# A new order for the first 480 entries of a hand-ordered gated-attention and MLP kernel, with GpSimd's steps there on VectorE

## The chip, the cores and the metric

One core of a Trainium2 chip runs the whole kernel. TensorE multiplies matrices into PSUM, VectorE and ScalarE work element by element, GpSimd is another element-wise engine, and SyncE (SP) issues the DMA transfers. Each engine takes its instructions from a queue of its own, strictly in the order in which the program issued them, and waits at an instruction until the data of other engines is there. The metric is the device time of one execution in microseconds; the median of three runs counts.

## The reference

```python
def _attn_ref(q, k, v, f_logit):            # 4 x 8 heads, 768 steps, 48 wide
    f = 1.0 / (1.0 + np.exp(-f_logit))
    for t in range(S):
        state = f[:, :, t, :, None] * state + einsum('bhd,bhe->bhde', k[:, :, t], v[:, :, t])
        y[:, :, t] = einsum('bhd,bhde->bhe', q[:, :, t], state)

def _moe_ref(x, w_in, w_out):               # 3072 tokens, 384 -> 2048 -> 384
    h = x @ w_in
    g = h * np.clip(h + 3.0, 0.0, 6.0) / 6.0
    return g @ w_out
```

The output of the gated attention, reshaped to 3072 tokens of 384 numbers, is the input `x` of the MLP.

## The kernel before

The sequence of 768 steps is cut into 6 chunks of 128, so there are 24 units (4 batches, 6 chunks); unit `i` is batch `i % 4` of chunk `i // 4`, and the units of one chunk make up one group of 512 tokens for the MLP. The state of each batch is carried from chunk to chunk.

A unit runs through these steps, each named in the order list with the unit's number. SP loads its gates (`load`), queries and keys (`loadq`) and values (`loadv`). ScalarE takes the sigmoid (`gate`). VectorE scans the gates backwards (`back`, line 428) and multiplies the keys (`kmul`, line 441), takes the reciprocal of the chunk's decay (`rend`, lines 444 and 445), scans forwards (`fwd`, line 448) and multiplies the queries (`qmul`, line 454). TensorE transposes the keys (`tk`, line 516; ScalarE copies the result, `ktok`), makes the keys-by-values products (`kv`, line 537), the queries-by-keys products (`att`, line 497), which VectorE masks (`mask`, line 504), and from them and the state the output (`qs`, line 571, and `av`, line 587). `carry0`, `carry1` and `decay` (line 457) pass the state on, from chunk 1 on by VectorE. ScalarE copies the output as a 16-bit number (`xh`); `xs` (line 612, TensorE) and `xl` add its rest for the first units; `hole` is a DMA that moves some rows of it.

The weights arrive in 16 blocks (`ld.f`, 768 KB each) and are turned into a 16-bit upper part and a 16-bit rest by ScalarE (`z`, `cy`, `high`) and VectorE (`mid`, line 301, `dif`, line 308, `top`, line 312, and `low`, or its halves `lowi` and `lowo`, line 320).

The MLP of block `f` for a group is `mm1` (9 matmuls, TensorE), `relu` (ScalarE), `g` (VectorE), `gh` (ScalarE) and `gl` (VectorE, line 693) and `mm2` (9 matmuls). For the first blocks of the first group it is cut in halves of two units each: `mm1a`, `relua`, `ga` (line 841), `mm2a` for units 0 and 1, and the same with `b` for units 2 and 3. In the first group, `mm2a`, `mm2b` and `mm2x` read the 32-bit weights. `warm.n` multiplies a blank tile into an unused bank, n times 128 columns (line 1071); its result is read by nobody.

The order of all this is a list written out in the program: `ORDER`, 1559 entries. An entry is a step, its number and, for steps that write to one of the five PSUM banks shared by attention and MLP, the bank (0 to 3 the halves of two pairs, 4 the single one; for `att`, `kv` and `qs` the number says which half of which pair). The loop at line 1063 calls the steps in the list's order, and lines 1088 and following hold each engine's queue to it. The order of two entries on different engines doesn't matter, except through banks and buffers. Gates have 3 buffers, so `load.3` waits until unit 0's scans are done, and `load.4` until unit 1's are; raw weights have 3 buffers, queries and values 4. `ON_POOL` names the steps that `engine()` (line 373) puts on GpSimd instead of VectorE; there are 15, all in the first 433 entries.

Of the kernel before, what the change touches and what calls it, by code (L numbers as in the profile page):

```python
# [63 lines left out]
mm2a.1 ktok.4 loadv.4 ld.3 cy.3 z.3 hole.2 mid.2 dif.2 top.2 att.4.2 kv.4.3 hole.3 mm1b.0.0 high.2 back.5 mid.3  # L64
relub.0 loadq.5 mm1b.1.1 relub.1 lowi.2 gb.0 dif.3 kmul.5 rend.5 gb.1 mm1a.2.4 mm1b.2.0 top.3 mm2b.0 mm2b.1 fwd.5
tk.5.1 relua.2 relub.2 gb.2 qmul.5 ld.4 z.4 cy.4 mid.4 mm2b.2 high.3 ktok.5 lowi.3 ga.2 mm1b.3.0 load.6 gate.6 loadq.6
dif.4 back.6 top.4 load.7 mm1a.3.4 ld.5 relub.3 mm2a.2 relua.3 ga.3 high.4 gb.3 cy.5 z.5 mask.4 mm2a.3 lowi.4 mm1a.4.1
relua.4 rend.6 ld.6 mm1b.4.4 relub.4 loadv.6 gate.7 loadq.7 mm2b.3 carry0.4 kmul.6 fwd.6 mid.5 ga.4 dif.5 z.6 qmul.6
top.5 cy.6 tk.6.1 ktok.6 mm2a.4 back.7 ld.7 decay.5 high.5 qs.4.2 decay.6 att.5.0 gb.4 av.4 kv.6.1 carry1.4 lowi.5
mm1.5.4 mask.5 mm2b.4 carry0.6 xh.4 z.7 xl.4 mid.6 dif.6 kmul.7 carry1.6 loadv.5 kv.5.3 ld.8 relu.5 g.5 mm2x.5 cy.7  # L70
top.6 high.6 cy.8 rend.7 tk.7.0 mid.7 dif.7 load.8 lowi.6 carry0.5 top.7 mm1.6.4 ktok.7 qs.5.2 fwd.7 qmul.7 high.7
loadv.7 relu.6 g.6 z.8 decay.7 att.6.0 ld.9 lowi.7 gate.8 av.5 cy.9 z.9 mask.6 mm1.7.4 relu.7 mid.8 dif.8 top.8 mid.9
carry1.5 dif.9 high.8 low.8 mm2x.6 mm1.8.0 g.7 loadq.8 ld.10 top.9 xh.5 cy.10 relu.8 high.9 back.8 rend.8 mm2x.7 ld.11
xl.5 g.8 att.7.2 z.10 cy.11 qs.6.0 kv.7.3 mid.10 load.10 loadv.8 av.6 dif.10 low.9 top.10 z.11 mid.11 gh.8 mm1.9.4
ld.12 ld.14 xh.6 xl.6 gl.8 mm2.8 dif.11 high.10 low.10 relu.9 g.9 cy.12 mm1.10.1 top.11 mask.7 kmul.8 carry0.7 gh.9
gl.9 hole.4 relu.10 high.11 mm2.9 carry1.7 g.10 low.11 z.12 mid.12 ld.13 dif.12 top.12 cy.13 gh.10 gl.10 tk.8.1 ktok.8
mm1.11.0 z.13 high.12 qs.7.2 mm2.10 av.7 loadq.9 ld.15 kv.8.3 decay.8 relu.11 mid.13 dif.13 low.12 loadv.9 mm1.12.1
g.11 gh.11 xh.7 top.13 carry0.8 high.13 xl.7 hole.7 gl.11 relu.12 z.14 z.15 low.13 fwd.8 qmul.8 mm2.11 g.12 gh.12
mm1.13.4 relu.13 g.13 cy.14 gh.13 gl.13 gl.12 mm2.12 cy.15 qs.8.2 mid.14 dif.14 att.8.0 mask.8 lowo.0 top.14 high.14
hole.6 hole.5 mm1.16.4 load.9 mid.15 mm1.17.1 relu.16 carry1.8 relu.17 dif.15 ws1.0 g.16 mm1.20.0 g.17 loadq.11 low.14  # L80
gate.10 xtop.0 gate.9 mm1.18.1 load.11 top.15 relu.18 loadq.10 back.9 high.15 gh.16 av.8 back.10 mm1.14.4 g.18 mm2.13
lowo.4 gh.17 relu.14 low.15 g.14 gh.14 mm1.15.1 mm1.19.4 lowo.6 gh.18 kmul.9 gl.18 rend.9 relu.15 g.15 lowo.3 gh.15
# [1 line left out]
mm2.16 gate.11 lowo.2 ws2.0 relu.19 od.0 ws3.0 mm2.17 rend.10 xh.8 g.19 back.11 od.2 kmul.10 relu.20 decay.9 relu.23
kmul.11 hole.8 fwd.10 rend.11 od.1 load.13 qmul.10 xsum.0.2 g.20 g.23 mm1.21.4 relu.21 load.12 xleast.0 tk.10.3 ws4.0
qmul.9 decay.10 ktok.10 mm2.18 gh.19 g.21 mm1.25.3 gh.20 mm1.24.2 gh.21 loadv.10 gate.12 wtop.4 gl.19 relu.24 att.9.1
relu.25 kv.9.0 gl.20 fwd.11 g.25 carry0.9 loadv.12 g.24 wsh.0 load.14 qmul.11 mm1.22.4 gate.13 relu.22 back.12 gh.24
mm2.19 tk.11.3 gl.21 ws1.1 mask.9 gh.23 carry1.9 ktok.11 mm2.20 g.22 qs.9.0 att.11.3 gate.14 loadq.12 gh.25 gl.25 av.9
att.10.2 mm2.21 back.13 gh.22 xh.9 gl.23 kv.11.0 rend.12 kv.10.1 gl.22 mask.10 loadq.13 decay.11 mm1.26.4 ws2.1
mask.11 carry0.10 qs.10.3 ws3.1 carry0.11 carry1.10 kmul.12 kmul.13 fwd.12 qs.11.1 av.10 av.11 relu.26 mm2.22 ws4.1  # L90
xh.10 xh.11 decay.12 rend.13 mm1.27.3 gl.24 carry1.11 relu.27 loadq.14 decay.13 fwd.13 tk.12.2 mm1.28.1 relu.28 hole.9
ktok.12 wsl.0 ws1.2 g.27 tk.13.0 mm2.23 qmul.12 qmul.13 wsh.1 hole.10 att.13.3 ws2.2 g.26 ktok.13 g.28 xtop.1 att.12.1
t0.4 loadv.13 kv.12.2 kv.13.0 back.14 carry0.13 load.15 hole.11 load.16 xsum.1.4 carry0.12 gh.26 mm2.24 gh.27 mm2.25
t0.5 mask.13 carry1.12 t1.4 t1.5 seed.0.2 kmul.14 mm1.30.3 gh.28 t2.4 ws3.2 xleast.1 carry1.13 t2.5 th.4 ws4.2 gate.15
mask.12 gl.26 gl.27 wsl.1 th.5 ws1.3 mm2.26 tl.4 mm1.29.1 tk.14.2 relu.30 mm1.31.0 tl.5 relu.29 rend.14 g.30 p1.8.4
loadv.14 ktok.14 ws2.3 relu.31 p7.8.2 g.29 wsh.2 cs.8 ca.8.2 loadv.17 mm2.27 g.31 p6.8 gh.29 gate.16 fwd.14 qs.13.0
xtop.2 cx.8.3 qs.12.1 p2.8 wsl.2 ws3.3 ra.8 back.15 gl.28 p5.8 av.13 av.12 mm2.28 gh.31 gaw.8 loadq.15 loadq.17 gh.30
ws4.3 rend.15 load.17 ce.8 wsh.3 p4.8 qmul.14 gl.30 gl.29 xh.13 xh.12 p3.8 p8.8 rb.8 rx.8 p7.9.1 decay.14 wsl.3 mm2.29
gl.31 kmul.15 loadq.16 re.8 tk.15.0 gew.8 cs.9 p1.9.4 gbw.8 ca.9.2 mm2.30 fwd.15 loadv.15 gxw.8 back.16 ktok.15
xsum.2.1 mm2.31 p6.9 qmul.15 p7.11.0 xmost.2 gh.33 gh.34 cs.11 xleast.2 p2.9 decay.15 gl.34 hole.13 gh.32 kv.15.1  # L100
kv.14.0 kmul.16 cx.9.3 gl.32 outs.5 load.18 ra.9 hole.12 carry0.14 carry1.14 p4.9 carry0.15 outs.3 carry1.15 p5.9 rx.9
att.14.0 gaw.9 att.15.1 ce.9 outv.4 gate.17 p8.9 mask.14 rend.16 p3.9 mask.15 gh.35 gate.18 qs.15.0 back.17 re.9
qs.14.1 gxw.9 fwd.16 kmul.17 gl.33 gl.35 mm2.32 av.14 av.15 gew.9 p7.10.3 xh.15 rend.17 loadq.18 mm2.33 mm2.34 t0.6
p1.10.4 rb.9 mm2.35 gbw.9 qmul.16 fwd.17 xh.14 loadv.16 back.18 gh.37 gh.38 rend.18 cs.10 decay.16 load.19 kmul.18
ca.10.2 gl.38 hole.15 p6.10 gh.36 tk.17.0 gl.37 p2.10 hole.14 decay.17 tk.16.1 gh.39 cx.10.3 gl.36 p4.10 t1.6 gate.19
fwd.18 ra.10 gaw.10 t2.6 ktok.17 p5.10 ktok.16 att.16.0 kv.16.1 mm2.36 ce.10 t0.7 qmul.17 p8.10 load.20 rx.10 re.10
load.21 qmul.18 back.19 loadv.18 p3.10 mm2.37 rb.10 mask.16 gew.10 carry0.16 carry1.16 p1.11.4 gbw.10 gh.40 att.17.0
gxw.10 kv.17.1 t1.7 th.6 loadq.19 ca.11.2 gl.40 gl.39 mm2.38 gh.42 p6.11 t2.7 carry0.17 xtop.3 carry1.17 gl.42 gate.21
wtop.3 th.7 p2.11 rend.19 tl.6 mm2.39 cx.11.3 gate.20 mm2.40 mask.17 ra.11 gaw.11 tl.7 p4.11 gh.43 rx.11 p5.11 ce.11
tk.18.1 p7.13.0 p8.11 gh.41 gxw.11 gl.43 ktok.18 cs.13 gl.41 xsum.3.3 wtop.8 p3.11 qs.17.1 rb.11 qs.16.0 mm2.41  # L110
loadq.20 re.11 av.17 xmost.3 loadv.19 av.16 xleast.3 p7.12.3 gbw.11 gh.46 gew.11 xh.16 gh.45 p1.12.4 ca.12.2 xh.17
gl.45 mm2.42 loadv.23 att.18.1 kv.18.0 decay.18 gh.44 p2.12 p6.12 back.20 gl.46 cs.12 mm2.43 cx.12.3 carry0.18 gl.44
# [1126 lines left out]
```

## Time and profile before

| what | value |
|---|---|
| median of 3 runs | 459.32 us (459.2 to 459.85) |
| the profiled execution | 459.1 us, of which 457.4 us are its span |
| TensorE matmuls, busy | 449.4 us, 98% of the span |
| VectorE, busy | 359.3 us, 79% |
| ScalarE, busy | 231.2 us, 51% |
| GpSimd, busy | 19.0 us, 4%, all in the first 105 us |

The span is the time from the first to the last instruction of that one execution. [...] The letters at an idle time name the engine and line that ended it.

### The profile page before, as it was taken

Reading aid. Unit: us, or ns where it says so; the run is one execution under the profiler, and the core shown is the slowest. Engines: PE = TensorE matmul, PEld = TensorE weight load, DVE = VectorE, ACT = ScalarE, POOL = GpSimd, SP = SyncE. Lnnn points to the kernel's source line nnn. Section 1 sums busy time; section 2 is a strip of 40 time slices with the busy share of each in tenths; the row PEclk is TensorE's granted clock in tenths of the full one; section 3 lists DMA queues with packets and bytes.
Section 4 is the critical chain, followed back from the end, with each engine's and each line's share of the span. In section 5 each row is a group of like instructions: output and inputs, shape, how many; then the busy total and the mean of one; then the engine's idle time right before and its main releaser. Section 6 shows DMA issues by size and latency. Waiting matters only on the chain.

```text
span 457.4 us, 12555 instructions
## 1 busy us (share of the span) xinstructions
PE 449.4 (98%) x5445; PEld 292.8 (64%) x5449; DVE 359.3 (79%) x643; ACT 231.2 (51%) x389; POOL 19.0 (4%) x31
## 2 busy tenths in 40 slices
...
GB/s 283 223 251 385 225 189 251 203 155 16 52 125 99 158 52 59 108 3 120 89 1 85 78 142 18 21 143 2 1 10 1 5 29 2 1 115 2 1 0 73
DMA packets 25531, 43.18 MB, mean 94 GB/s; under 512 B 2560, under 2 KB 17408, under 8 KB 25472
## 3 DMA queue, kind: packets, MB, share of 16 engines
...
q10 hardware_dynamic: 1600, 0.79, 0.6%
q14 instruction: 16, 0.13, 0.1%
...
## 4 chain that ended last, share of the span: by engine, by line
PE 94%; DVE 2%; DMA 1%; ACT 1%; issue 0%; SPq 0%; ACTq 0%
PE o L709 35%; PE pair L772 16%; PE single L772 9%; PE pair L664 7%; PE single L664 5%; PE o L846 3%; PE pair L497 3%; PE pair L587 3%; PE pair L571 3%; PE pair L537 2%; PE o L720 2%; PE pair L516 2%; PE o_half L862 1%; PE pair L862 1%; PE single L828 1%; PE pair L828 1%
## 5 line engine op out<-in xcount | busy, mean ns | idle before, releaser
L709 PE MATMUL o<-gg,weight 128*128 128x512 f16 x744 | 173.5, 379 | 0.1
L709 PEld LDWEIGHTS <-weight 128*128 128x128 f16 x744 | 71.7, 98 | 73.8
L772 PEld LDWEIGHTS <-weight 128*128 128x128 f16 x672 | 65.1, 98 | 13.3 <-issue 0.2
L772 PE MATMUL pair<-xmem,wide 128*128 128x256 f16 x384 | 51.2, 273 | 0.1
L683 ACT ACTIVATE gg<-raws 128x512 f16<-128x512 f32 x64 | 38.4, 624 | 23.9 <-DVE raws L806 8.1
L772 PE MATMUL single<-xmem,weight 128*128 128x256 f16 x384 | 49.8, 273 | 0.2 <-DVE raws L806 0.2
L801 ACT ACTIVATE raws<-pair,half 128x512 f32<-128x512 f32 x32 | 21.5, 684 | 42.7 <-PE pair L772 33.7
L772 PEld LDWEIGHTS <-wide 128*128 128x128 f16 x384 | 36.9, 98 | 8.7 <-DVE single L787 0.6
L801 ACT ACTIVATE raws<-single,half 128x512 f32<-128x512 f32 x32 | 22.0, 687 | 40.0 <-PE single L772 32.4
L664 PEld LDWEIGHTS <-weight 128*128 128x128 f16 x243 | 23.1, 98 | 26.8 <-issue 0.3
L772 PE MATMUL pair<-xmem,weight 128*128 128x256 f16 x288 | 36.5, 273 | 0.0
L806 DVE SCALAR_TENSOR_TENSOR raws<-raws,single 128x512 f32<-128x512 f32 x32 | 21.8, 682 | 18.4 <-ACT raws L801 18.4
L693 DVE TENSOR_TENSOR gg<-raws,gg 128x512 f16<-128x512 f32 x48 | 31.9, 682 | 5.0 <-ACT gg L683 5.0
L664 PE MATMUL pair<-xmem,weight 128*128 128x512 f16 x144 | 33.2, 379 | 0.0
L787 DVE TENSOR_TENSOR pair<-pair,raws 128x512 f32<-128x512 f32 x16 | 11.2, 697 | 25.5 <-PE pair L772 17.2
L806 DVE SCALAR_TENSOR_TENSOR raws<-raws,pair 128x512 f32<-128x512 f32 x32 | 21.5, 681 | 12.3 <-ACT raws L801 12.1
L448 DVE TENSOR_TENSOR_SCAN suffix<-gates,rend 112x516 f32<-112x516 f32 x24 | 29.7, 1236 | 0.1
L428 DVE TENSOR_TENSOR_SCAN suffix<-gates,unit 112x516 f32<-112x516 f32 x23 | 28.1, 1224 | 0.5 <-ACT gates L422 0.5
L664 PE MATMUL single<-xmem,weight 128*128 128x512 f16 x99 | 23.2, 380 | 0.1
L674 ACT ACTIVATE tg<-pair,half 128x512 f32<-128x512 f32 x16 | 10.9, 687 | 19.5 <-PE pair L664 16.3
L683 ACT ACTIVATE gg<-tg 128x512 f16<-128x512 f32 x24 | 14.4, 626 | 9.1 <-DVE tg L678 5.2
L504 DVE TENSOR_TENSOR a<-pair,causal 128x512 f32<-128x512 f32 x24 | 16.3, 682 | 1.2 <-PE pair L537 1.2
...
## 6 DMA issues: line engine op xcount, KB each, us to landing
qkf<-qk SPq DMA_DIRECT2D x24, 512.0 KB, 4.9
...
```

The lines of the kernel that those rows point to most:

```text
L428: nc.vector.tensor_tensor_scan(flat(sf)[:, ::-1], gt[:, 1:][:, ::-1], flat(unit)[:, ::-1], 0.0, op0=ALU.mult, op1=ALU.add,)
L448: nc.vector.tensor_tensor_scan(flat(sf), gt[:, :NP * (C + 1)], flat(rend), 0.0, op0=ALU.mult, op1=ALU.add,)
L497: nc.tensor.matmul(d["at"][HC * odd:HC * (odd + 1), e, 2 * n + c], t[rs, 1, n, c, odd], t[rs, 0, n, c, odd], start=not growing[at], stop=T ...
L504: nc.vector.tensor_tensor(d["a"].rearrange("r p e t -> r e p t"), d["at"], causal.unsqueeze(1).unsqueeze(1).broadcast_to([128, 2, NP, HC]) ...
L571: nc.tensor.matmul(d["y"][to:to + 64, odd, n, cs], before[rs, p], t[rs, 0, n, c, odd], start=alone and (odd, e) not in seen, stop=False, s ...
L664: nc.tensor.matmul(h, win[:, f, a, k * 128:(k + 1) * 128], g["xt"][:, k, :g["n"] // C, b], start=i == 0, stop=i == 3 * KT - 1,)
L683: nc.scalar.activation(d["gg"][:, 0], d["t"], AF.Copy)
L693: engine("gl", int(g["name"]) * NF + f).tensor_tensor(d["gg"][:, 1], d["t"], d["gg"][:, 0], op=ALU.subtract)
L709: nc.tensor.matmul(g["o"][m], wout[:, f, a, m * 128:(m + 1) * 128], g[f]["gg"][:, b], start=f == 0 and i == 0, stop=f == NF - 1 and i == 2 ...
L772: nc.tensor.matmul(to[:, n * 256:(n + 1) * 256], weights(q, n, a), g["wide"][:, :, block - 3, b], start=fresh and count == 1, stop=count = ...
L801: nc.scalar.activation(to, src, AF.Relu, bias=half, scale=RISE)
L806: nc.vector.scalar_tensor_tensor(to, to, TOP, src, op0=ALU.min, op1=ALU.mult)
```

## The change

`ON_POOL` is emptied, so its 15 steps go to VectorE: `kmul` of units 1, 6, 7 and 8, `qmul` of unit 8, `decay` of units 4, 7 and 8, three `gl`, and four of the weights' steps. The first 471 entries of `ORDER` are replaced by 480. They are the same steps in another order and partly with other banks; only the warm entries differ, where one `warm.5` goes and ten `warm.1` are added (44 units of 128 columns in place of 39). From `mm2.14` on, 1088 entries are unchanged. The beginning and the last line of both parts:

```diff
 ON_POOL = """
-kmul.1 decay.4 kmul.6 lowi.5 kmul.7 decay.7 lowi.7 kmul.8 gl.9 decay.8 gl.11 qmul.8 gl.12 lowo.0 low.14
+
 """.split()
 ORDER = """
-load.0 loadh.0 gate.0 gateh.0 back.0 backh.0 loadq.0 loadv.0 rend.0 kmul.0 load.1 fwd.0 gate.1 back.1 warm.16 tk.0.3
-ktok.0 warm.4 kv.0.1 carry0.0 load.2 qmul.0 warm.1 att.0.0 loadq.1 ld.0 rend.1 qs.0.2 mask.0 gate.2 warm.1 av.0 xh.0
-kmul.1 tk.1.4 ktok.1 carry1.0 fwd.1 qmul.1 warm.3 att.1.0 xs.0 loadv.1 back.2 mask.1 rend.2 cy.0 load.3 warm.3 kv.1.3
-z.0 mid.0 loadq.2 gate.3 back.3 ld.1 carry0.1 warm.1 qs.1.0 dif.0 kmul.2 top.0 fwd.2 xl.0 carry1.1 loadq.3 av.1 hole.0
-tk.2.4 rend.3 xh.1 xs.1 xl.1 z.1 qmul.2 warm.5 att.2.2 kmul.3 cy.1 mid.1 fwd.3 ktok.2 loadv.2 high.0 warm.4 kv.2.1
-carry0.2 tk.3.4 ktok.3 mask.2 load.4 gate.4 qs.2.0 hole.1 av.2 xh.2 carry1.2 lowi.0 mm1a.0.4 relua.0 dif.1 qmul.3
-top.1 high.1 ga.0 loadv.3 xs.2 att.3.2 mask.3 kv.3.1 ld.2 carry0.3 carry1.3 lowi.1 xl.2 loadq.4 warm.1 qs.3.2 av.3
-xh.3 mm1a.1.4 cy.2 xs.3 xl.3 relua.1 z.2 back.4 kmul.4 rend.4 fwd.4 ga.1 decay.4 mm2a.0 qmul.4 load.5 gate.5 tk.4.1
...
-gl.14 gl.15 tk.9.1 lowo.5 lowo.1 mm2.14 fwd.9 mm2.15 gl.16 ktok.9 gl.17 outs.2 loadv.11 lowo.7 outv.1 outs.0 mm1.23.1
...
+load.0 loadh.0 gate.0 gateh.0 back.0 backh.0 loadq.0 loadv.0 rend.0 kmul.0 load.1 fwd.0 warm.16 loadq.1 tk.0.2 gate.1
+ktok.0 warm.4 warm.1 back.1 qmul.0 kmul.1 loadq.2 load.2 warm.1 kv.0.3 carry0.0 gate.2 warm.1 rend.1 att.0.1 tk.1.4
+loadv.2 loadv.1 mask.0 warm.3 load.3 fwd.1 warm.1 back.2 ktok.1 qmul.1 warm.1 carry1.0 ld.0 gate.3 kmul.2 qs.0.1
+kv.1.3 load.4 av.0 rend.2 loadq.3 carry0.1 att.1.2 back.3 xh.0 tk.2.4 z.0 carry1.1 qs.1.0 mask.1 warm.1 warm.1 gate.4
+ktok.2 warm.1 fwd.2 cy.0 xs.0 kmul.3 rend.3 av.1 xl.0 kv.2.3 mid.0 carry0.2 carry1.2 fwd.3 loadv.3 xh.1 dif.0 warm.1
+qmul.2 warm.3 qmul.3 ld.1 ld.2 tk.3.4 hole.0 top.0 xs.1 ktok.3 xl.1 warm.1 kv.3.2 att.2.1 att.3.0 cy.1 carry0.3 z.1
+high.0 mask.3 mid.1 hole.1 mask.2 qs.3.3 ld.3 cy.2 loadq.4 warm.4 z.2 av.3 qs.2.0 av.2 xh.3 xh.2 warm.1 dif.1 lowi.0
+top.1 warm.1 high.1 back.4 ld.4 xs.3 warm.1 mid.2 xs.2 mm1a.0.4 xl.2 relua.0 warm.1 lowi.1 dif.2 mm1a.1.0 carry1.3
+ga.0 xl.3 hole.2 mm2a.0 relua.1 top.2 cy.3 ga.1 high.2 z.3 kmul.4 hole.3 cy.4 z.4 rend.4 mm2a.1 load.5 lowi.2 tk.4.2
...
+gh.14 load.11 rend.9 gl.14 gl.15 back.10 lowo.5 mm1.20.0 av.8 tk.9.1 lowo.6 gh.18 gl.18 mm2.14 fwd.9 mm2.15 gl.16
...
 """.split()
```

In the old list `mm1a.0` stands between the attention steps of units 2 and 3, in the new one behind those of all four units. The steps of the first weight block on VectorE (`mid.0`, `dif.0`, `top.0`) come later there, and so does its load.

## Rows read from the trace of the kernel before

**Rows 1.** The page: busy time by engine, and the chain by engine

```profile
PE 449.4 (98%) x5445; PEld 292.8 (64%) x5449; DVE 359.3 (79%) x643; ACT 231.2 (51%) x389; POOL 19.0 (4%) x31
...
PE 94%; DVE 2%; DMA 1%; ACT 1%; issue 0%; SPq 0%; ACTq 0%
```

**Rows 2.** Stretches: start:end, length, then busy us per engine, clock, DMA share, GB/s

```profile
3.50:25.50 22.00, 19.43 (x428) 12.24 (x426) 20.83 (x34) 12.03 (x23) 1.66 (x2) 1.00 0.79 284
25.50:116.50 91.00, 90.87 (x1172) 56.88 (x1165) 81.98 (x142) 64.96 (x100) 14.81 (x14) 1.00 0.55 201
116.50:200.00 83.50, 83.40 (x1101) 49.24 (x1102) 79.16 (x143) 41.27 (x73) 0.00 (x0) 1.00 0.29 90
```

**Rows 3.** Timeline of TensorE: start, us, engine, line, operation, tiles, count

```profile
28.19 0.49 PE L1071 MATMUL idle<-blank 128*128 128x128 f32 x2
...
29.27 0.69 PE L587 MATMUL pair<-a,v 64*64 64x64 f32 x32
29.89 1.16 PE L828 MATMUL single<-xmem,weight 128*128 128x256 f16 x9
30.88 0.38 PE L612 MATMUL pair<-xmem,less 112*112 112x256 f16 x2
31.11 1.46 PE L846 MATMUL o<-th,wide 128*128 128x256 f32 x6
...
116.52 4.05 PE L709 MATMUL o<-gg,weight 128*128 128x512 f16 x18
```

**Rows 4.** Timeline of VectorE in the front, with the idle time ahead

```profile
9.79 1.16 DVE L444 TENSOR_SCALAR ends<-suffix 112x4 f32<-112x4 f32 x1
...
14.71 0.69 DVE L504 TENSOR_TENSOR a<-pair,causal 128x512 f32<-128x512 f32 x1
15.32 0.16 DVE L444 TENSOR_SCALAR ends<-suffix 112x4 f32<-112x4 f32 x1
...
15.61 0.35 DVE L301 TENSOR_SCALAR raws<-top 128x768 int16<-128x768 int16 x1
16.00 1.24 DVE L428 TENSOR_TENSOR_SCAN suffix<-gates,unit 112x516 f32<-112x516 f32 x1
17.15 0.53 DVE L308 TENSOR_TENSOR top<-top,raws 128x768 int16<-128x768 int16 x1
17.60 0.69 DVE L441 TENSOR_TENSOR qkf<-qkf,suffix 112x512 f32<-112x512 f32 x1
...
27.24 0.42 DVE L841 SCALAR_TENSOR_TENSOR th<-th,single 128x256 f32<-128x256 f32 x1 [0.97 <-ACT th L837]
```

**Rows 5.** VectorE's groups, 3.5 to 118.4 us: count, busy us, mean ns, idle before

```profile
L320 DVE TENSOR_TENSOR weight<-wide,weight 128x768 f16<-128x768 f32 x7 | 6.7, 952 | 0.2
...
L320 DVE TENSOR_TENSOR weight<-wide,weight 128x384 f16<-128x384 f32 x11 | 6.0, 552 | 0.2 <-ACT weight L317 0.2
...
L441 DVE TENSOR_TENSOR qkf<-qkf,suffix 112x512 f32<-112x512 f32 x6 | 4.1, 687 | 0.3 <-DMA qkf<-qk 0.3
...
L457 DVE TENSOR_TENSOR decayed<-state,ends 112x192 f32<-112x192 f32 x2 | 0.7, 350 | 0.0
```

**Rows 6.** Timeline of GpSimd, its first step behind the setup

```profile
9.50 1.42 POOL L441 TENSOR_TENSOR qkf<-qkf,suffix 112x512 f32<-112x512 f32 x1 [5.76 <-DMA qkf<-qk]
```

**Rows 7.** Timeline of SP's queue: the issue of `loadq.3`

```profile
8.96 0.44 SPq L413 DMA_DIRECT2D qkf<-qk  x1
```

**Rows 8.** The page's DMA issues: count, KB each, median us to landing

```profile
qkf<-qk SPq DMA_DIRECT2D x24, 512.0 KB, 4.9
```

**Rows 9.** VectorE's waits, 25.5 to 118.4 us: total us, times, longest

```profile
DVE tg L678 <- ACT tg L674: 4.5, 6, 2.4
```

**Rows 10.** Timeline of VectorE behind 116.5 us

```profile
118.39 1.23 DVE L448 TENSOR_TENSOR_SCAN suffix<-gates,rend 112x516 f32<-112x516 f32 x1
...
147.43 0.36 DVE L552 TENSOR_TENSOR middle<-pair,decayed 112x192 f32<-112x192 f32 x1 [0.47 <-PE pair L537]
```

**Rows 11.** Timeline of TensorE at `qs.10`

```profile
149.26 0.46 PE L571 MATMUL pair<-qkf,decayed 48*64 48x64 f32 x16
```

More of the change, by code (lines that the diff above doesn't have):

```diff
@@ L64 @@
[L64 to L82, printed above, removed]
-gl.14 gl.15 tk.9.1 lowo.5 lowo.1 mm2.14 fwd.9 mm2.15 gl.16 ktok.9 gl.17 outs.2 loadv.11 lowo.7 outv.1 outs.0 mm1.23.1
@@ L84 @@
[L84 to L112, printed above, removed]
-mask.18 p4.12 ra.12 p5.12 kmul.19 fwd.19 gaw.12 gh.47 mm2.44 decay.19 load.22 ce.12 loadv.22 od.5 back.21 carry1.18
```

120 lines of the change are left out of this document (84 added, 36 removed).

## The prediction

> **What bounds the kernel now.** I read the page first: TensorE's matmuls cover 449.4 us of a span of 457.4 us, and the chain that ended last lies on TensorE for 94% [rows 1]. A covered TensorE is still not a useful one, because the `warm` entries, matmuls on a blank tile, count as busy too. So I cut the span into stages [rows 2]. From 3.5 to 25.5 us TensorE shows 19.43 us busy of 22.0, but its work there waits for VectorE, which is busy for 20.83 us of the 22.0. From 25.5 to 116.5 us TensorE has 0.13 us uncovered, VectorE is busy for 81.98 of 91.0 us, GpSimd for 14.81. From 116.5 to 200 us VectorE is at 79.16 of 83.5. The granted clock is 1.00 in each of these stretches. So there is time to gain for TensorE ahead of about 31 us alone; behind it TensorE runs one matmul after the other, and all that can happen there is that a gain is kept or lost.
>
> I therefore took two marks in TensorE's rows. `mm2a.0` starts at 31.11 us [rows 3]. In both lists the same real TensorE steps stand ahead of it (four units of attention, `xs.0` to `xs.3`, `mm1a.0`, `mm1a.1`), so its start tells what the front costs. `mm2.14` starts at 116.52 us [rows 3]; from there on both lists are the same word for word, so the shift at that mark is the shift of the end, as long as VectorE is shifted too.
>
> **Part 1: the front.** `mm2a.0` reads what `ga.0` writes, the VectorE step at 27.24 us [rows 4]. I counted VectorE's list up to `ga.0` in both orders. The new one has everything that the old one has, and six steps more: `kmul.1` (from GpSimd), `mask.3`, `back.4`, `mid.2`, `lowi.1` and `dif.2`. A step's price is the distance from its start to the next one's, about 0.08 us below its duration: the mask at 14.71 us lasts 0.69 and is followed 0.61 later, `mid` takes 0.39, `back` 1.15, `dif` 0.45 in that way [rows 4]; the multiply and the half-tile `lowi`, less 0.08, are 0.60 and 0.47 [rows 5]. So 0.60 + 0.61 + 1.15 + 0.39 + 0.47 + 0.45 = 3.67 us are added ahead of `ga.0`.
>
> Against that stand two holes in the old front. At 9.79 us a VectorE step on 4 elements per row takes 1.16 us, where the same step takes 0.16 at 15.32 us [rows 4]; it ends as GpSimd's `kmul.1` ends, which runs 1.42 us from 9.50 [rows 6]. With GpSimd out of the way I take 0.98 us of it back. And VectorE waits for 0.97 us ahead of `ga.0` [rows 4], because it is there before TensorE and ScalarE are; the six steps fill that. One new wait I see: the mask of unit 0 now comes when VectorE has been free for a short time and `att.0` is just ending; I take 0.2 us. So `ga.0` starts at 27.24 + 3.67 - 0.98 - 0.97 + 0.2 = 29.16 us and `mm2a.0` at about 29.65. That is **1.46 us ahead** of 31.11.
>
> Is TensorE there by then? Counting back from `ga.0` by the same prices, the last mask ends at about 24.85. In the old front an `av` and its `xs` start 1.61 us apart (29.27 and 30.88), `xs` takes 0.23 and `mm1a` 0.99 [rows 3]; with a warm entry of 0.5 between two `mm1a` that gives 24.9 + 1.6 + 0.2 + 1.0 + 0.5 + 1.0 = 29.2. So VectorE sets this start, and TensorE has 0.4 us in hand. The new list has 44 units of warm matmuls in place of 39; all but the last three lie where TensorE waits for VectorE anyway. These three are in the 0.4 us; without that cover each would cost up to 0.53 us, the distance from the warm entry at 28.19 us to its successor [rows 3].
>
> DMA: `ld.0` now stands behind `load.3`, which waits for the first unit's scan, so it goes out at about 8 us; `mid.0`, its first VectorE user, comes at about 19 us by the same count. `loadq.3` stands behind `load.4`, which waits for `fwd.1`; it goes out at about 13 us instead of 8.96 [rows 7] and, at 4.9 us to landing [rows 8], is there at 17.9. VectorE reaches `kmul.3` at about 18.3. So nothing is lost in the count, and at most some 0.5 us if the transfer is slower. What is queued on SP behind `load.4` (`loadv.3`, `ld.1`, `ld.2`, `hole.0`) has its users later still.
>
> **Part 2: the dense stretch, 31 to 116.5 us.** TensorE's steps are the same here. VectorE gets 14 more from GpSimd: 3 `kmul`, 1 `qmul` and 3 `gl` at 0.60, 3 `decay` at 0.27, 3 half-tile `low` at 0.47, the full one at 0.87; 4.2 + 0.8 + 1.4 + 0.9 = 7.3 us [rows 5], in place of 14.8 us on GpSimd [rows 2]. VectorE is idle for 9.02 us here [rows 2], 0.97 of them already used; the largest group of its waits, 4.5 us, is for ScalarE's part of the gate and so for TensorE [rows 9]. Each wait also costs the 0.08 us of overlap, a dozen times: some 9.1 us lost behind 27.24. From there to `fwd.9`, a step at the start of the common part, at 118.39 us [rows 10], VectorE works 91.15 - 9.1 = 82.0 us; in the new order 82.0 - 3.1 (moved ahead of `ga.0`) + 7.3 = 86.2 us. TensorE needs 116.52 - 31.11 = 85.4. **Both engines are then full**, and VectorE would reach `fwd.9` at 29.16 + 86.2 = 115.4 us if it never waited, 3.0 us earlier than now.
>
> Of these 3.0, 1.5 are the shift that I want to keep and 1.5 are all that VectorE may wait on its way. I counted both new lists forward with these prices, need by need. With a shift of 1.5 TensorE's results come at most 0.4 us late for a VectorE step (`g.15`), since VectorE, with more to do, comes later to each. In the other direction VectorE has about 1.0 us in hand at the closest places behind `mm2a.0` (`att.6`, `mm2.12`). So I expect waits of 0.5 to 1.5 us and a loss of 0 to 0.5; waits on ScalarE that I did not count would add to it. I take 0.15, nearer to no loss, since the reserve of 1.0 lies between.
>
> **Part 3: from 116.5 us on.** The list is the same. A tight place is `qs.10` at 149.26 us [rows 11], whose last VectorE input, `carry0.10`, ends at 147.43 + 0.36 = 147.79 [rows 10]: 1.5 us in hand. VectorE and TensorE arrive earlier by about the same, so nothing changes.
>
> **The sum.** -1.46 + 0.15 = -1.3 us. The profiled execution took 459.1 us (a span of 457.4 and 1.7 around it), the median is 459.32; the same 1.3 off gives 457.8 and **458.0 us**.
>
> **The rivals.** *VectorE becomes the bound (slower).* Place: the dense stretch. With 86.2 us of work beside 85.4, each wait of VectorE beyond about 1.0 us delays TensorE by as much, so the front is used up at 1.0 + 1.5 = 2.5 us of waits. For it: the old order has some 9 us of them; if 3.5 to 6 us stay, the end comes 1 to 3.5 us late, at 460.3 to 462.8. Against it: most of the old waits are VectorE being early, which 7.3 us of added work cures. [...]
> *The gain is given back.* Waits of 1.6 to 3.4 us leave the time at 458.4 to 460.2, about 459.3. A front that doesn't move because `loadq.3` or ScalarE holds the first units up by 1.5 us ends here too.
> *More than forecast.* The 0.2 us of new wait and the 0.15 of loss don't come, and VectorE, no longer beside GpSimd, has other steps shortened as the one at 9.79 us was: with another 1 us in the stretch the sum is -2.7, 456.6.
>
> **How the numbers follow.** A measurement can tell about 0.2%, 0.92 us, from no change. Forecast (456.9 to 458.4): 0.50. More (below 456.9): 0.08. Given back (458.4 to 460.2): 0.24. VectorE the bound (above 460.2): 0.18. So faster 0.58, same 0.24, slower 0.18. The range from 456.6 to 460.6 leaves out some 0.05 below and 0.15 above.
>
> **What would show it.** `mm2a.0` near 29.6 us, no wait of VectorE ahead of `ga.0` and no 1.16 us step near 10 us (part 1). VectorE busy for about 88 of 91 us between 25 and 116 us, and `fwd.9` near 116.5 (part 2). `mm2.14` near 115.2, with the same distance to the end as now, 340.9 us (part 3). I am wrong if `mm2a.0` doesn't move, or if it moves and TensorE then shows pauses that end with VectorE's `gl`, `low` or `qmul` steps, or if the granted clock falls below 1.00 in the front, where I take it as unchanged.

## The result and the profile after

The changed kernel takes 463.44 us (median of 4 runs, 462.12 to 463.6), the kernel before 459.26 beside it: a ratio of 1.009, interval 1.0077 to 1.0102. It is 4.2 us **slower**. The forecast was 458.0 us, with a range up to 460.6; the prediction was wrong.

The profiled execution of the changed kernel takes 463.39 us, its span 461.6. The page's busy times and its chain by engine, to be laid beside [rows 1]:

```profile
PE 451.9 (98%) x5465; PEld 296.6 (64%) x5465; DVE 363.9 (79%) x658; ACT 230.6 (50%) x389; POOL 2.7 (1%) x16
...
PE 96%; issue 1%; DVE 1%; DMA 1%; ACT 0%; SPq 0%; ACTq 0%
```

The edit did what its diff says: GpSimd is empty but for its setup. "issue" in the chain has gone from 0% to 1%. The three stretches, columns as in [rows 2]:

```profile
3.50:25.50 22.00, 17.91 (x373) 12.94 (x373) 18.38 (x30) 10.48 (x22) 0.23 (x1) 0.97 0.79 290
25.50:116.50 91.00, 90.39 (x1169) 57.59 (x1164) 85.43 (x153) 63.70 (x98) 0.00 (x0) 0.99 0.58 200
116.50:200.00 83.50, 83.50 (x1090) 47.92 (x1088) 79.98 (x145) 40.61 (x69) 0.00 (x0) 1.00 0.29 90
```

In the front TensorE is busy for 1.5 us less than before and VectorE for 2.4 us less, and the granted clock is no longer 1.00. Neither engine is fully busy there, so something else holds them up. The marks, and what stands ahead of them, in TensorE's timeline (columns as in [rows 3], in brackets the idle time ahead and what ended it):

```profile
15.05 0.46 PE L497 MATMUL pair<-qkf 48*64 48x64 f32 x14 [0.57 <-DVE qkf L454]
15.97 0.50 PE L497 MATMUL pair<-qkf 48*64 48x64 f32 x18 [0.47 <-issue]
...
18.93 0.87 PE L537 MATMUL pair<-v,ktok 64*64 64x48 f32 x48
22.84 1.03 PE L1071 MATMUL idle<-blank 128*128 128x128 f32 x4 [3.05 <-issue]
...
25.12 1.42 PE L537 MATMUL pair<-v,ktok 64*64 64x48 f32 x46
...
34.41 2.83 PE L846 MATMUL o<-th,wide 128*128 128x256 f32 x12
37.08 0.55 PE L516 MATMUL pair<-ident,qkf 112*128 112x112 f32 x4
38.15 1.03 PE L828 MATMUL pair<-xmem,weight 128*128 128x256 f16 x8 [0.52 <-DMA xmem<-xmem]
...
120.80 1.46 PE L709 MATMUL o<-gg,weight 128*128 128x512 f16 x6
```

`mm2a.0` starts at 34.41 us, not 31.11 [rows 3] and not 29.65 as forecast. `mm2.14` starts at 120.80, 4.28 us later than before; from there to the end of the span it is 340.8 us (340.9 before). So nearly everything is lost ahead of `mm2a.0` (3.30 us), and 0.98 us behind it.

The two rows that end with "issue" (a time in which the engine waited for nothing that the profile shows) are the clue. `att.1` (line 497) stops after 14 of its 32 matmuls, in the middle of a step. Behind `kv.2` TensorE is idle for 3.05 us and then goes on with a warm entry, a matmul that waits for nobody. The profile names no semaphore that ended either pause, which suggests that TensorE had no instructions; the runs below test that. Numbering TensorE's records in the trace from 0, its weight loads and the entries of its queue (waits and the like) included, it stops ahead of record 449 and ahead of record 705, which is 256 further. From here on a block is such a stretch of 256 records, and a pause is counted with the weight loads as work: 0.47 and 2.93 us (the 3.05 of the row is between matmuls alone). VectorE has the pause on its list as a wait for TensorE's `att`, ahead of the next mask:

```profile
28.16 0.69 DVE L504 TENSOR_TENSOR a<-pair,causal 128x512 f32<-128x512 f32 x1 [4.35 <-PE pair L497]
```

What was under way meanwhile, in stretches (columns as above) and in the issues of SP's queue:

```profile
18.00:20.00 2.00, 1.79 (x85) 1.67 (x84) 1.83 (x5) 1.33 (x3) 0.00 (x0) 1.00 1.06 431
20.00:22.00 2.00, 0.00 (x0) 0.00 (x0) 2.00 (x4) 0.90 (x3) 0.00 (x0) 1.00 1.02 417
24.00:26.00 2.00, 2.00 (x43) 1.77 (x43) 0.00 (x0) 1.62 (x3) 0.00 (x0) 0.51 0.03 8
26.00:28.00 2.00, 2.00 (x101) 2.00 (x96) 0.00 (x0) 1.41 (x4) 0.00 (x0) 0.64 0.34 49
```

```profile
13.26 0.33 SPq L409 DMA_DIRECT2D gates<-fg  x1
13.63 1.29 SPq L413 DMA_DIRECT2D qkf<-qk  x1
14.97 0.43 SPq L418 DMA_DIRECT2D v<-v  x1
15.44 0.91 SPq L284 DMA_DIRECT2D raws<-w  x2
```

Between 13.3 and 16.4 us SP issues `load.4`, `loadq.3`, `loadv.3`, `ld.1` and `ld.2`, some 2.5 MB; from 18 to 22 us the 16 DMA engines are full (share 1.06 and 1.02). The profile lists a fetch of instructions as a packet among those of the DMA engines, on a queue of its own: here it starts at 20.52 us and ends at 21.46, and TensorE goes on 1.38 us later. The table of DMA queues for 16 to 20.4 us has no such packet, the one for 20.4 to 22.9 us has it (queue, kind: packets, MB, share):

```profile
q8 instruction: 1, 0.02, 2.3%
```

In the kernel before the same fetch starts at 17.46 us, while the DMA engines are almost idle (share 0.11 from 16 to 18 us), and TensorE comes to record 705 only at 23.14 us. After the long pause the granted clock falls to 0.50, from about 24.0 to 27.4 us (0.51 and 0.64 in the two stretches).

### The profile page after: what moved, and what is told of

It reads as the page before. It is cut to its first block, busy times and chain, and to the rows that moved or that the text cites. A ratio compares the mean times of both kernels' runs of the same rounds, so it can differ in the third digit from the quotient of the medians.

```text
span 461.6 us, 12579 instructions
## 1 busy us (share of the span) xinstructions
PE 451.9 (98%) x5465; PEld 296.6 (64%) x5465; DVE 363.9 (79%) x658; ACT 230.6 (50%) x389; POOL 2.7 (1%) x16
## 4 chain that ended last, share of the span: by engine, by line
PE 96%; issue 1%; DVE 1%; DMA 1%; ACT 0%; SPq 0%; ACTq 0%
PE o L709 35%; PE pair L772 16%; PE single L772 9%; PE pair L664 7%; PE single L664 4%; PE pair L497 3%; PE idle L1071 3%; PE pair L587 3%; PE pair L571 3%; PE pair L537 2%; PE o L846 2%; PE o L720 2%; PE pair L516 2%; PE pair L828 2%; PE pair L862 1%
## 5 line engine op out<-in xcount | busy, mean ns | idle before, releaser
L772 PEld LDWEIGHTS <-weight 128*128 128x128 f16 x672 | 65.1, 98 | 13.3 <-issue 0.2
L664 PEld LDWEIGHTS <-weight 128*128 128x128 f16 x243 | 23.1, 98 | 27.7 <-issue 0.8
L664 PE MATMUL pair<-xmem,weight 128*128 128x512 f16 x153 | 35.2, 379 | 0.0
L787 DVE TENSOR_TENSOR pair<-pair,raws 128x512 f32<-128x512 f32 x16 | 11.2, 697 | 25.5 <-PE pair L772 17.2
L674 ACT ACTIVATE tg<-pair,half 128x512 f32<-128x512 f32 x17 | 11.6, 688 | 22.9 <-PE pair L664 18.8
L664 PE MATMUL single<-xmem,weight 128*128 128x512 f16 x90 | 21.1, 380 | 0.0
L1071 PE MATMUL idle<-blank 128*128 128x128 f32 (+2 forms) x44 | 15.0, 471 | 4.2 <-issue 3.0
```

Of the source, the lines that this page charges most:

```text
L664: nc.tensor.matmul(h, win[:, f, a, k * 128:(k + 1) * 128], g["xt"][:, k, :g["n"] // C, b], start=i == 0, stop=i == 3 * KT - 1,)
L772: nc.tensor.matmul(to[:, n * 256:(n + 1) * 256], weights(q, n, a), g["wide"][:, :, block - 3, b], start=fresh and count == 1, stop=count = ...
L1071: nc.tensor.matmul(idle[:, :n * 128].rearrange("p (a n) -> p a n", n=128), blank, blank.unsqueeze(1).broadcast_to([128, n, 128]), start=Tr ...
```

## The experiments

Theory T1: the new order brings TensorE to the ends of its instruction blocks early, while the loads that the order bunches keep the fetches back; the pauses and the low clock behind them are the loss. Rivals: T3, the order of the compute steps is bad in itself; T4, VectorE cannot carry GpSimd's work (there is no T2). Times are medians, ratios against the kernel before, which took 458.5 to 459.0 us beside them.

**The two halves of the change.** e2: order of before, `ON_POOL` emptied. e3: new order, `ON_POOL` of before.

> The order of before, with GpSimd's operations of the first part on VectorE: that half of the change alone. T1 (a pile of loads in the new order): the fetch of TensorE's instructions stays at about 17.5 us, no pause of 3 us that ends with an issue; VectorE gets about 8 us more work in an order that was not made for it, of which its waits can take about half, so 459.5 to 463. T4 (VectorE's added work alone is the cause): 463 or more.

> The new order, with GpSimd's operations of before back on GpSimd: the other half of the change alone. T1: the four transfers are bunched as in the changed kernel, so the pause of some 3 us and the low clock stay, mm2a.0 at 33 to 35 us, time 462 to 464.5. T4 (VectorE's added work is the cause): with that work on GpSimd the time returns to 457.5 to 459.5.

e2: 463.16 us (1.0112, 1.0086 to 1.0137), at the edge between its two expectations. `mm2a.0` at 30.87 us, no pause; but `mm2.14` at 120.12, so 89.25 us between them in place of 85.41. TensorE's longest waits between 3 and 120 us (total, times, longest):

```profile
PE o L709 <- DVE gg L693: 1.8, 1, 1.8
PE pair L497 <- DVE qkf L454: 1.6, 2, 0.8
PE o L709 <- ACT gg L683: 0.5, 1, 0.5
```

e3: 463.6 us (1.0097, 1.0077 to 1.0117), with pauses of 0.96 and 2.64 us ahead of records 449 and 705, `mm2a.0` at 35.64. So in the old order VectorE's added work costs 3.8 us, in the new order none: taking it away (e3) gains nothing, and from `mm2a.0` to `mm2.14` e3 takes 86.55 us where the changed kernel takes 86.39. T4 falls for the changed kernel.

**Moving loads.** e1: `ld.1` behind `ld.0`, `ld.2` behind `hole.0`. e4: `ld.2` behind `hole.0` alone:

```
-qmul.2 warm.3 qmul.3 ld.1 ld.2 tk.3.4 hole.0 top.0 ...
+qmul.2 warm.3 qmul.3 ld.1 tk.3.4 hole.0 ld.2 top.0 ...
```

e5: e4, and SP waits with `ld.1` for `mask.1` and with `ld.2` for `qmul.2` (a semaphore on SP's DMA, no other engine touched).

> The new order with two entries of SP's list moved: ld.1 right behind ld.0, ld.2 right behind hole.0; nothing moves on a compute engine. Theory T1 (in the new order SP issues loadq.3, loadv.3, ld.1 and ld.2 within 3 us, the fetch of TensorE's next instructions stands behind them, TensorE runs out of instructions for 3.05 us and then runs 3.4 us at a granted clock near 0.5): the fetch goes through before 19.5 us, no pause of 3 us that ends with an issue, granted clock 1.0 between 24 and 28 us, mm2a.0 at 29.9 to 30.8 instead of 34.41 us, time 457.8 to 459.5. Theory T4 (VectorE's added work is the cause) and T3 (the order of the compute steps is the cause): mm2a.0 stays above 33.5 us, time 462 to 464.

> The new order with ld.2 alone moved behind hole.0, so that three of the four transfers stay bunched. T1: the fetch comes about 1 us earlier than in the changed kernel, the pause is 1 to 2.5 us instead of 3.05; mm2a.0 lies between that of e1_loads_spread and 34.41 us; if the clock falls only after a longer pause, nearer to the first: time 458 to 462. T3 and T4: no change, 462 to 464.

> The order of e4_ld2_later, with two waits added for SP: ld.1 is issued when VectorE has done mask.1, ld.2 when it has done qmul.2; nothing else changes. T1, sharpened (TensorE's instructions come in blocks of 256; it stops ahead of its instructions 449 and 705 when the block's fetch stands behind loads): the fetch that went at 18.53 us in e4_ld2_later goes before 17.3 us, the stop ahead of instruction 705 (1.29 us there) is gone, the one ahead of 449 (0.94 us there) stays, granted clock 1.0 throughout the front; mm2a.0 at 30.2 to 30.9 us, time 458.2 to 460. T3 (the order of the compute steps is the cause): mm2a.0 not below 31.5 us, 460 or more.

e4: 461.6 us (1.0069, 1.005 to 1.0088). e5: 460.57 us (1.0048, 1.0029 to 1.0066). e1: 462.44 us (1.007, 1.0048 to 1.0092). Of the three, e5 alone is clear of the changed kernel's interval (1.0077 to 1.0102); those of e4 and e1 overlap it. TensorE's timeline of e4, then e5 (line numbers of e5 are 4 higher, the warm entry's 13):

```profile
15.76 0.50 PE L497 MATMUL pair<-qkf 48*64 48x64 f32 x18 [0.94 <-issue]
...
20.98 1.03 PE L1071 MATMUL idle<-blank 128*128 128x128 f32 x4 [1.40 <-issue]
...
31.77 1.53 PE L846 MATMUL o<-th,wide 128*128 128x256 f32 x6
```

```profile
16.37 0.50 PE L501 MATMUL pair<-qkf 48*64 48x64 f32 x18 [0.96 <-issue]
...
20.21 1.04 PE L1084 MATMUL idle<-blank 128*128 128x128 f32 x4
...
25.27 0.45 PE L575 MATMUL pair<-qkf,middle 48*64 48x64 f32 x13 [1.04 <-issue]
...
32.31 1.53 PE L850 MATMUL o<-th,wide 128*128 128x256 f32 x6
```

The second fetch started 4.55 us after TensorE's record 449 in the changed kernel, 2.76 in e4, 1.26 in e5, as `ld.2`, then `ld.1` too, left its way; the pause ahead of record 705 went from 2.93 to 1.29 to nothing. No compute step moved, and in the profiled executions `mm2a.0` came 2.6 and 2.1 us earlier, so the order of the compute steps alone does not make the loss. But e5 has a new pause, ahead of record 961, again 256 further. That `ld.1` now meets the third fetch is one reading of it, and not shown: in e11 below the third fetch is as late with the DMA engines nearly idle. The rest of the expectation for e5 failed: `mm2a.0` at 32.31 and 460.57 us are what it gave for T3. e1 failed as a whole: `mm2a.0` is at 35.64 us, later than in the changed kernel. Its first fetch came late (pause of 1.50 us ahead of 449), the clock was 0.50 from 17.5 to 24.3 us, and 0.81 us ahead of 961 is the third fetch again. The trace is that of its slowest execution (464.6 us, the others 460.92 to 462.9).

**Making room for all fetches.** e6: `loadq.3` held until `mask.0`, `ld.0` behind `load.4`, `loadv.3` and `ld.1` late. e8: `loadq.2` held until `mask.0`, `loadv.2` behind `loadq.3`, `ld.1` held until `mask.1`, `ld.2` until `qmul.3`. e9: e8 with `ld.1` held until `back.3`. e10: e8 with `ON_POOL` of before.

> The new order with the loads of the front spread so that both fetches find room: loadq.3 behind load.3 and not before mask.0 is done, ld.0 behind load.4, loadv.3 and ld.1 not before mask.1 is done and mask.1's wait alone for both, ld.2 behind hole.0 and not before qmul.2 is done. T1: the first fetch starts before 12.5 us, the second before 17.5 us, neither stop ahead of instruction 449 nor ahead of 705 is left, mm2a.0 at 29.3 to 30.2 us (29.65 was the forecast for the changed kernel), mm2.14 at 115.0 to 116.0, time 457.3 to 458.8, that is 0 to 1.2 us less than before. T3 and T4: mm2a.0 above 31.5 us and 460 or more.

> The new order with SP's loads laid so that each of three fetches finds room: loadq.2 behind ld.0 and not before mask.0 is done, loadv.2 behind loadq.3, ld.1 not before mask.1, ld.2 behind hole.0 and not before qmul.3. T1: first fetch before 13.0 us (request at about 10.9), second before 17.7, third before 22.3; what is left of stops ahead of TensorE's instructions 449, 705 and 961 is below 0.5 us in sum, granted clock 1.0; mm2a.0 at 29.4 to 30.4 us, time 457.5 to 459.2. T3 (order of the compute steps) and T4 (VectorE's added work): mm2a.0 above 31.5 us, time 460 or more.

> e8_room_two with GpSimd's operations of before back on GpSimd: that half of the change alone, where no stop hides it. By the prediction's first and second part, VectorE's step beside kmul.1 becomes longer again by up to 1 us in the front, and VectorE has 7.9 us less work: mm2a.0 0 to 1 us later than in e8_room_two, dense stretch the same within 0.5 us, time 0 to 1.2 us above e8_room_two. If VectorE's added work cost time there (T4), this kernel is faster than e8_room_two by 1 us or more.

e6 (465.6 us), e8 (462.6) and e9 (462.31) failed. The first fetch of e6 did go at 12.00 us and its pause was gone, but ScalarE's `z.0` stood 4.14 us for `ld.0`, with `carry1.1` and so VectorE's mask behind it; in e8 `kmul.2` stood 1.81 us for `loadq.2`:

```profile
16.61 0.69 DVE L446 TENSOR_TENSOR qkf<-qkf,suffix 112x512 f32<-112x512 f32 x1 [1.81 <-DMA qkf<-qk]
```

Both ran at a granted clock of 0.50 for 6.8 us (from 20.9 us in e6, from 17.0 in e8). In these versions what was moved out of a fetch's way was itself late. e10 differs from e8 in `ON_POOL` alone. Its 463.26 us lie 0.66 above e8, as expected, within the spread of both (461.84 to 463.35 and 461.88 to 465.68); from `mm2a.0` to `mm2.14` it takes 86.55 us, e8 86.58. So there too VectorE's added work costs nothing that can be seen. `mm2a.0` is 1.36 us later, more than expected, with longer pauses (0.81 and 0.59 us, in e8 0.27), so the front of e10 says nothing on the halves.

**Loads taken away.** e11 and e12: `ld.0`, `ld.1`, `ld.2` are not transferred; GpSimd fills the three buffers with a constant (three blocks of weights are not the input's), in the new and in the old order.

```
-        nc.sync.dma_start(out=raw[:, 1:4 * WN + 1], in_=w[f].bitcast(I16))
+        if f < 3:
+            nc.gpsimd.memset(raw.bitcast(F32), 1.1269397735595703)
+        else:
+            nc.sync.dma_start(out=raw[:, 1:4 * WN + 1], in_=w[f].bitcast(I16))
```

> The changed kernel without the transfers of ld.0, ld.1 and ld.2 (2.3 MB of the 6.4 MB of the front): GpSimd fills those three weight buffers with a constant instead, so the first three blocks of weights are not those of the input, and nothing else differs. T1: with less in the queues the first two fetches go within 2 us of their request, no stop of more than 0.5 us ahead of TensorE's instructions 449, 705 and 961, granted clock 1.0; mm2a.0 at 29.3 to 30.4 us (forecast of the changed kernel: 29.65), time 457.3 to 459.0. T3 (order of the compute steps) and T4 (VectorE's added work): mm2a.0 above 31.5 us, 460 or more. GpSimd's fills lie beside VectorE's first steps and may lengthen them by up to 1 us.

> The kernel before with the same edit: ld.0, ld.1 and ld.2 replaced by fills on GpSimd. T1: it has no stop to lose, so mm2a.0 stays at 30.8 to 31.5 us and the time at 458.2 to 459.6; e11 is then faster than this one by 0.3 to 1.5 us. If the loads slowed both orders alike, it gains as much as e11 does against the changed kernel.

e11: 460.46 us (1.0037, 1.0022 to 1.0052), `mm2a.0` at 31.93, both outside T1's expectation and inside that of T3. Pauses of 0.46 and 0.49 us, clock 1.00:

```profile
20.90 1.03 PE L1074 MATMUL idle<-blank 128*128 128x128 f32 x4 [0.58 <-issue]
...
25.40 0.45 PE L574 MATMUL pair<-qkf,middle 48*64 48x64 f32 x13 [0.50 <-issue]
...
31.93 1.40 PE L849 MATMUL o<-th,wide 128*128 128x256 f32 x4
```

GpSimd's fills (4.02 us from 3.66) held VectorE's first steps up (that of line 447 took 2.88 us), and `att.0` started at 11.74 us, 1.72 us later than before; from `att.0` to `mm2a.0` it took 20.19 us, where before took 21.09 and the changed kernel 23.81. So without the three weight loads the new front is the shorter one, by 0.9 us, and by 1.9 if the two pauses are taken off. This is what speaks against T3, although e1, e5, e6, e8, e9 and e11 all came out where the expectations had put T3 (`mm2a.0` above 31.5 us, 460 us or more): taken without its pauses, and in the changed kernel without the low clock, the time from `att.0` to `mm2a.0` is 19.6 us in the changed kernel and e4, 19.8 in e5 and 19.2 in e11. That is a subtraction: the one version of the new order without pauses, e6, waited for its loads instead. e11's third fetch started 2.29 us after record 705 though the DMA engines were nearly idle (share 0.09 from 20.9 to 23.1 us): the transfers were not all that delayed a fetch here, and the new order paused without them too. e12 is no control: two of the fills ran behind GpSimd's `kmul.1`, and VectorE's step of line 447 lasted as long (rows of VectorE, then GpSimd); TensorE then idled from 11.55 to 14.37 us, and the granted clock was 0.50 from 14 to 20 us (462.68 us; two of its ten executions took 458.95 and 459.24).

```profile
9.72 3.79 DVE L447 TENSOR_SCALAR ends<-suffix 112x4 f32<-112x4 f32 x1
```

```profile
9.47 1.38 POOL L444 TENSOR_TENSOR qkf<-qkf,suffix 112x512 f32<-112x512 f32 x1 [4.42 <-DMA qkf<-qk]
10.79 2.69 POOL L285 MEMSET raws<- 128x1538 f32 x2
```

**The old order under pressure.** e7: before, with `ld.2` right behind `ld.1`. e14: before, with `load` and `loadq` fetching the 112 rows that are used in place of 128. e15: e4 with the same.

> The kernel before with one entry of SP's list moved: ld.2 right behind ld.1, so that 768 KB more are issued at about 9 us, ahead of the fetch that goes at 13.79 us there; no compute step moves. T1: that fetch goes 0.8 to 2 us later, TensorE stops ahead of its instruction 449 for 0.3 to 2 us with no release that the profile shows, mm2a.0 up to 1 us later, time 458.5 to 460. If loads ahead of a fetch do not hold it up: no stop there, mm2a.0 at 31.0 to 31.2, time as before.

> The kernel before, with load and loadq fetching the 112 rows that are used instead of 128 (an eighth less of both, in all units): the control for e15. T1: no stop before, none now, mm2a.0 within 0.4 us of 31.1, time within 0.6 us of before.

> e4_ld2_later with load and loadq fetching 112 rows instead of 128, so that some 0.4 MB less (1 us of the DMA engines' time) stands ahead of the second fetch. T1: the second fetch starts 0.5 to 1.2 us earlier against its request than in e4_ld2_later (2.76 us there), the stop ahead of instruction 705 shrinks from 1.29 to 0.1 to 0.8 us, the one ahead of 449 from 0.94 to 0.2 to 0.8; mm2a.0 at 30.2 to 31.3 us, time 458.0 to 460. T3 and T4: as e4_ld2_later, 461 to 462.

e7: 458.84 us (1.0005, 0.9996 to 1.0015): the fetch started 3.39 us after record 193 (3.35 before), so the 768 KB more did not hold it back, and T1's expectation failed; the pause ahead of record 449 is 0.31 us, and the waits behind it took it up (`mm2a.0` 31.22). The fetch ended at 15.18 us, and both weight blocks issued ahead of it landed later (17.03 and 18.88): this fetch did not wait for all that was issued before it, and its delay here did not go by the bytes issued ahead of it alone. e14 and e15 went the wrong way, 462.19 and 463.15 us: the shorter transfers were the slower ones here. From 8 to 10 and 12 to 14 us, e14 (before moved 422 and 431 GB/s there, and between the two stretches 391 against 377 in e14):

```profile
8.00:10.00 2.00, 1.81 (x52) 0.97 (x50) 1.98 (x3) 1.06 (x2) 0.00 (x0) 1.00 1.04 287
12.00:14.00 2.00, 1.78 (x39) 1.19 (x38) 1.97 (x3) 0.97 (x3) 0.10 (x1) 1.00 1.06 304
```

That made e14 a better test than it was meant to be: its first fetch started at 15.49 us in place of 13.79, and the old order stopped ahead of the same record, 449, which is other work there, the 33rd matmul of `kv.1`:

```profile
15.97 0.68 PE L537 MATMUL pair<-v,ktok 64*64 64x48 f32 x32
17.97 0.44 PE L537 MATMUL pair<-v,ktok 64*64 64x48 f32 x16 [1.32 <-issue]
```

VectorE also waits 4.2 us for `qkf` loads in e14, where it waited 0.3 before (3 to 120 us); how the rest of the loss divides was not worked out.

**Shifting the count.** e16 (and e17, on e4): the first warm entry's four matmuls cut into 32. e18: replaced by 15 of 64 columns, 22 records more.

> The changed kernel with the four matmuls of the first warm entry (512 columns each) cut into 32 of 64 columns: the same columns, 56 instruction records of TensorE more ahead of all real work, nothing else. If TensorE's instructions come in blocks of 256 by count (T1), the two stops move with the count: still ahead of records 449 and 705, which are now other work: the first in av.0 (line 587) instead of the end of att.1 (line 497), the second within kv.2 (line 537) instead of the warm entry behind it; each still ends 1.3 to 1.6 us after the end of a fetch; their sum 2.5 to 5 us, time 461.5 to 465. If the stops belong to those places of the order (a semaphore, a buffer, VectorE), they stay at the end of att.1 and ahead of the warm entry behind kv.2.

> The changed kernel with the four matmuls of 512 columns of the first warm entry replaced by 15 of 64 columns, which at the 0.22 us each that they took in e16_count_shifted last about as long: 22 instruction records of TensorE more ahead of all real work. If TensorE's instructions come in blocks of 256 by count (T1): stops, where there are any, ahead of records 449 and 705 by the new count, which are the instructions 22 earlier in the work: the first within the front half of att.1, the second within kv.2 (line 537) and no longer ahead of the warm entry behind it; time 461 to 465. Otherwise the stops stay where they were.

e16 and e17 (473.21 and 469.42 us) shifted more than the count: the small matmuls took 0.22 us each and `tk.0` started 7 us late. They had no pause ahead of 449 and 705; e16 paused ahead of 961 and 1217, e17 ahead of 1217. e18 (465.03 us) was 2 us late at `att.0`, and had no pause ahead of 449 and 705, where one was expected; it had them at the next two block ends, records 961 and 1217, the second on work (`mm1a.0`) that paused in no other kernel:

```profile
26.02 0.50 PE L497 MATMUL pair<-qkf 48*64 48x64 f32 x18 [0.46 <-issue]
...
32.59 2.10 PE L828 MATMUL single<-xmem,weight 128*128 128x256 f16 x9 [1.75 <-issue]
```

Over the traces of all 20 kernels there are 26 pauses of more than 0.2 us, up to record 1217, that nothing in the profile ended. All stand ahead of record 449, 705, 961 or 1217, on six different lines of work, and all end 1.08 to 1.59 us after the end of a fetch packet. That the pauses follow the count and the fetch in these kernels is shown by this.

**The step beside GpSimd.** e19: before, with `kmul.1` alone on VectorE.

> The kernel before with one of GpSimd's operations, kmul.1, on VectorE. By the prediction's first part: VectorE's 1.16 us step beside it shrinks to 0.16, which gives back 0.98 and costs 0.60, so 0.4 us on VectorE up to mask.0; mm2a.0 0 to 0.4 us earlier than 31.11, time 458.3 to 458.9 where before has 458.8. If that step's length has nothing to do with GpSimd: VectorE 0.6 us later, mm2a.0 31.1 to 31.7.

459.34 us (1.001, 1.0001 to 1.0019). The step of line 444 takes 0.16 us, where it took 1.16 [rows 4]:

```profile
10.01 0.16 DVE L444 TENSOR_SCALAR ends<-suffix 112x4 f32<-112x4 f32 x1
```

The stall is real and goes with `kmul.1`; the end does not come earlier, and `mm2a.0` is at 32.09, later than expected. The rows show where the gain went. VectorE now waits 0.68 us for `att.0` ahead of the mask, where it had no wait, and `kmul.1` follows ahead of `qmul.1`, for which TensorE waits ahead of `att.1` (e19's mask and `att.1`, then `att.1` before):

```profile
11.05 0.69 DVE L504 TENSOR_TENSOR a<-pair,causal 128x512 f32<-128x512 f32 x1 [0.68 <-PE pair L497]
14.48 0.69 PE L497 MATMUL pair<-qkf 48*64 48x64 f32 x32 [0.80 <-DVE qkf L454]
...
13.88 0.69 PE L497 MATMUL pair<-qkf 48*64 48x64 f32 x32 [0.19 <-ACT state L557]
```

So `att.1` starts 0.60 us later, 0.21 of it because `att.0` did in that execution (10.23). A pause of 0.22 us ahead of record 961 is on the way to `mm2a.0` as well.

No version beat the kernel before.

## Why the prediction was wrong

**Part 1, the front, failed**, at two sentences. "So nothing is lost in the count, and at most some 0.5 us if the transfer is slower", and that what is queued behind `load.4` "has its users later still": each load was held against its own reader, and none against what else uses the DMA engines. And "TensorE has 0.4 us in hand": TensorE was counted as if it always had its instructions. What was left out was TensorE's instruction fetch: 3.40 us of pauses in the changed kernel. "So VectorE sets this start" did not come out either: in e4, e5 and e11 VectorE waits 0.22, 0.21 and 0.38 us right ahead of `ga.0` for ScalarE, which is behind TensorE's `mm1a.0` (e4's row below). The changed kernel has no wait there, but VectorE had waited 4.35 us at a mask before. What was right in it: the stall beside `kmul.1` went (0.16 us at 10.32), and `loadq.3` held nobody up by more than 0.2 us (it landed at 18.75, `kmul.3` started at 18.84).

```profile
31.21 0.42 DVE L841 SCALAR_TENSOR_TENSOR th<-th,single 128x256 f32<-128x256 f32 x1 [0.22 <-ACT th L837]
```

How far off, from the trace: 29.65 as forecast, plus 0.58 us because `att.0` started at 10.60 in that execution (10.02 before), plus 0.47 and 2.93 us of pauses, plus 0.78 us of low clock (from `tk.3` to `mm2a.0` 10.71 us, in e4 at full clock 9.93), makes 34.41; measured 34.41. To the hundredth this is luck: 29.65 is VectorE's count, the pauses are TensorE's. The same sum for e4 is 29.65 - 0.10 + 2.23 = 31.78 (31.77), for e5 29.65 + 0.49 + 2.00 = 32.14 (32.31), for e11 29.65 + 1.72 + 0.95 = 32.32 (31.93). Forecast and pauses together thus hold to 0.4 us in these four; the term left out was worth 3.40 us of pauses and 0.78 of clock. The sum does not hold where loads were late for other reasons (e6, e8, e9), and what the low clock cost e1, e3 and e15 was not worked out.

**"The granted clock ... I take it as unchanged"** was named as a condition, and it fell: it was 0.50 for 3.4 us, beginning 1.2 us behind the end of the 2.93 us pause, and took 0.78 us of the loss.

**Part 2, the dense stretch, was right in kind.** From `mm2a.0` to `mm2.14` it takes 86.39 us (85.41 before), 85.74 in e4 and 85.70 in e5; the loss was put at 0.15, it is 0.3 there. In the changed kernel 0.52 us more is `mm1b.1` waiting for a `hole` transfer. VectorE is busy for 85.43 of 91 us, not 88, because its wait of 4.35 us reaches into that stretch, to 28.16 us; in e4 it is 87.92.

**Part 3** was right: 340.8 us from `mm2.14`, 340.9 before.

**The rivals.** *VectorE becomes the bound* has the right sign and the wrong mechanism: it is what e2 shows for the old order (TensorE waits 1.8 us for a `gl`), not for the new one. *Given back* named a front held up by `loadq.3` or ScalarE, near to the cause but not it. What the count lacked stands in the traces: the pauses are at places 256 records apart (449, 705, 961, 1217), and of the 80 fetches for the blocks that start there 77 start only once TensorE is in the block before, the other three up to 47 records ahead of it. In the traces of the kernel before and of the changed one, with 10950 and 10991 records of TensorE, it comes to 43 block starts, at record 193 and every 256 from there, and either page lists 43 fetch packets (`q8 instruction: 43, 0.70 MB`). The pauses at two of these starts cost 3.40 us.

By these rows the old front was safe by its slowness: its blocks up to 449 and 705 took 5.76 and 6.93 us, so a fetch 3.35 us late was just in time (TensorE was at record 449 1.46 us after the fetch's end). The new front is faster through its blocks. Up to 449 the changed kernel takes 4.97 us, 0.47 of it the pause: its first fetch came earlier than before (2.46 us behind record 193 in place of 3.35), and TensorE still had to stop for it. The block up to 705 takes 3.85 us where nothing stops it (e5), and there the fetch was just in time: 1.26 us until its packet started, 1.05 for the packet, and 1.54 later TensorE was at record 705. In the changed kernel the same three were 4.55, 0.94 and 1.38.

What stays open: what sets a fetch's start (in e11 2.29 us behind record 705 with the DMA engines nearly idle, in the kernel before 0.24 us behind it with their share at 0.82 from 22 to 24 us). That the bunched loads held the second fetch back is what e4 and e5 show; for the first, e6 and e11 point the same way (0.86 and 0.90 us behind record 193, in the changed kernel 2.46); for the third it is not shown. Open is also the time of the new order without pauses and without late loads, which no run reached. The median of e4 lies 1.5 us above its profiled execution; whether its pauses were longer in the other executions, no trace shows.
